# Two steps' values and two steps' scores in one TensorE run for the last two blocks, a second buffer for the turned probabilities, six ring buffers, and a new table of due times

## The chip, the core and the metric

The kernel runs on one core of one Trainium2 chip. The metric is the device time of one execution in microseconds (us). Engines are named as in the profile: PE is TensorE, DVE is VectorE, ACT is ScalarE, POOL is GpSimd, SP is SyncE, which here only issues DMA transfers.

## What is computed

A banded attention over 8 batches, 8 heads, 576 positions and a head size of 64, followed by a feed-forward layer with 512 inputs, 2048 hidden units and 512 outputs over all 4608 tokens:

```python
scores = scale * np.matmul(q, k.transpose(0, 1, 3, 2))
mask = (rel >= 0) & (rel < window)          # rel = query position - key position, window = 64
attn = softmax(np.where(mask, scores, -1e9))
x = np.matmul(attn, v)                      # heads joined: 4608 x 512
h = x @ w_in                                # 512 -> 2048
g = np.where(h >= 1, h, np.where(h <= -1, 0.0, (h + 1) ** 2 / 4))
out = g @ w_out                             # 2048 -> 512
```

## The kernel before, in words

Attention goes in 36 steps of 128 queries, 4 per tile of 512 tokens. A step has four parts. `att_scores` on PE (line 422, in short S) multiplies queries and keys of all heads: 64 small matmuls in the trace from step 5 on. `att_masked`, `att_exp`, `att_inverse` and `att_normalize` on DVE, ACT and sometimes POOL make probabilities of them. For steps from 5 on `att_turn` (DVE, line 491), `att_write` and `att_read` (SP, lines 502 and 505) transpose these: they are written to one tensor `moved` in DRAM and read back into one buffer, `turned` (named `ptd` in the profile). `att_values` on PE (line 535, in short V) multiplies them by the values: 32 small matmuls in the trace.

The feed-forward layer of the first three tiles runs straight: `ffn_in` (line 1139) and `ffn_out` (line 1185). The other six tiles go in three blocks of two tiles (`add_super`), each by a scheme with 7 products where plain blocking needs 8. `ffn_product` (line 914) makes 56 products of 6 matmuls for the first layer, `out_product` (line 1000) 56 more for the second. The scheme's weight operands lie in DRAM (`kept`), and each product reads one of them, 256 KB, through a ring of SBUF buffers (`ring_load`, line 894; `ring=7` in `BUFS`). Its input operands are sums and differences of attention outputs, made in `add_build` (lines 570 and 606) when both steps r and r+4 of a block are there, so the steps go in the order `A_ORDER` = 0, 4, 1, 5, 2, 6, 3, 7.

Nothing is ordered by hand. Every piece of work is put into a list (`plan.add`) with a key, a cost for each engine that could do it, what it needs and which buffers it takes. `Plan.run` then lays the pieces out one by one: on each engine the piece that can start first, among those about equally early the one with the lowest key. Keys come from the constants at the top of the file. What comes out is a fixed order of instructions on each engine; on the chip each engine goes through its own in that order and waits where an operand is missing. SP too: a transfer that waits holds up all transfers behind it.

Before the change a late step puts on PE one piece, V of an older step and S of its own (`do` in `add_step`); the last two steps' V of a block stand alone, and so do the first two S. The attention of a block runs on PE between the products of the block before.

Of the kernel before, what the change touches and what calls it, by code (L numbers as in the profile page):

```python
# [10 lines left out]
F32 = mybir.dt.float32  # L11
F32R = mybir.dt.float32r
# [30 lines left out]
E_SPAN = 5.91  # L43
E_LEAD = 17.1
W_LEAD = -23.43
W_FIRST = (41.07, 11.15, 26.87, -10.88, -31.72)
W_STEP = 25.17
L_LEAD = -2.38
W_LATE = (3.63, -16.39, 9.21, 20.15, 0.56)
V_LATE = 14.51  # L50
W0_KEY = -103.61
FIRST_LOAD = 0, (0,)
M_LATE = 5.76
W0_STEP = 8.68
FINE = 4
NWARM = 8
A_FIRST = (-100.35, -96.85, -96.18, -80.14)
A_NEXT = 10.78
A_STEP = 5.01
A_SPAN = 18.65  # L60
A_LEAD = 5.32
O_LAG = 2.91
# [11 lines left out]
B_DUE = (4.53, -27.23, 1.18)  # L74
B_STEP = 13.93
B_FIRST = -15.42
A_END = 2.75
V_PE = 1270
NORM = dict(Pool=800, DVE=480), dict(DVE=610)
G_LATE = (11.92, 0.97, -5.01, 12.64, 1.72)  # L80
D_LATE = (-2.36, 0.62, 26.98, 2.89, 13.75, 21.44)
TURN = 965, 1500
# [4 lines left out]
SUM_KEEP = 880  # L87
V_LATE_2 = 43.01
LAND = 800
WRITE = 1140  # L90
BACKLOG = 2500
MOVED = 3700
PATIENCE = dict(ACT=300, DVE=0, Pool=303, PE=0, SP=0)
BUFS = dict(qt=2, kt=2, vt=4, ps_a=2, sm=2, ptd=3, pt2=1, x=2, u=2, ps_h=2, a=2, gh=2, gl=2, acc=4, o=2, tmp=2)
BUFS.update({n: 1 for n in ("xtmp", "xs0", "xs1", "xs2", "xs3", "xs4", "xs5", "X", "Y")}, raw=4, ring=7, op=5)

# [4 lines left out]
S_LATE = 5.22  # L101
S_PACE = 47.29
O_CHANGE = (-1.18, 7.84, 12.31)
EARLY_2 = 3.64
A_SUPER = ((10.49, 4.41), (12.01, 4.44))
A_ORDER = (0, 4, 1, 5, 2, 6, 3, 7)
BUILD = (-17.42, 29.27)
# [5 lines left out]
R_LEAD = -10.33  # L113
R_LOAD = 370
L_DVE = 4, 6, 8
G_LEAD = (9.32, -1.73, 0.08, 4.82)
OP_LEAD = 45.65
D_LEAD = 1.02
# [6 lines left out]
class Plan:  # L125
# [29 lines left out]
    def run(self):  # L155
# [22 lines left out]
        for _ in self.work:  # L178
            best = None
            for e in engines:  # L180
# [12 lines left out]
                if could:  # L193
                    until = min(could)[0] + PATIENCE[e]
                    c = min((c for c in could if c[0] <= until), key=lambda c: c[1:])
                    best = c if best is None else min(best, c)
# [26 lines left out]
def banded_attention_then_ffn(ctx: ExitStack, tc: tile.TileContext, q, k, v, w, masks, out, out_t, dims):  # L223
# [26 lines left out]
    idt = const.tile([P, P], F32, name="idt")  # L250
    make_identity(nc, idt)
    msk = const.tile([P, 3, WIN], F32, name="msk")
# [89 lines left out]
    def w_low(g):  # L342
        t = ws[g]
        nc.vector.tensor_tensor(out=t[:, :, 1], in0=us[g], in1=t[:, :, 0].bitcast(F32), op=ALU.subtract)
# [3 lines left out]
    def add_weights(f, units):  # L348
# [6 lines left out]
        x = add(key - W_LATE[1], dict(ACT=act, DVE=67 + 1.05 * m), lambda e: w_top(g, e), [xr])  # L355
        x = add(key - W_LATE[2], dict(DVE=join), lambda e: w_join(g), [x])
        x = add(key - W_LATE[3], dict(ACT=high, DVE=30 + .6 * m), lambda e: w_high(g, e), [x])
        x = add(key - W_LATE[4], dict(DVE=low), lambda e: w_low(g), [x], gives=[("u", xr)])
# [145 lines left out]
    def att_read():  # L504
        nc.sync.dma_start(out=turned, in_=moved.rearrange("i k r j n -> (k r) i (j n)"))
# [19 lines left out]
    def att_values(s, pool):  # L525

        vt, pt = [vts.pop((s, i)) for i in range(2)], [ptd[pt_of(s, h)] for h in range(2)]
        vals[s] = ps = banks_of_heads(pool)
        for p in range(NP):
            for i in range(2):  # L530
                n = slice(i * QB, (i + 1) * QB)
                for h in range(2):
                    c = (2 * p + h) * D
                    w_ = turned[:, i].rearrange("p (j g n) -> p j g n", j=2, n=SQ)[:, :, h * NP + p] if s >= SOON else pt[h][:, p, n]
# [92 lines left out]
    def add_build(u, r, due, x0, x1):  # L627
# [3 lines left out]
        xs = i0  # L631
        for j in range(1, 4):
            xs = add(due, tt(2 * SB), lambda e, j=j: x_sums(r, j, e), [xs], shared=True)
        end = []
        for k in range(6):
            n = 4 * SB if k == 0 else 2 * SB
            after, slot, takes = [xs], f"xs{k}", []
# [9 lines left out]
            x = add(due, tt(n), lambda e, k=k: x_low(r, k, e), [x] + end, gives=gives, shared=True)  # L647
            end = [x]
            x_of[u, k].append(x)

    def add_step(t, i):
# [21 lines left out]
        xq = add(lk, dict(SP=390), lambda e: load_q(s), takes=["qt"], moves=packets(P, 4 * DM))  # L673
        xk = add(lk, dict(SP=480), lambda e: load_k(s) if s else None, takes=["kt"], moves=packets(P, 6 * DM) if s else None)
        vk, vc = lk + (V_LATE_2 if late else V_LATE), 450 if s < SOON else 640
        xv = add(vk, dict(SP=vc), lambda e: load_v(s, 0), takes=["vt"], moves=packets(P, 4 * DM), behind=last["v"])
        xw = add(vk, dict(SP=vc), lambda e: load_v(s, 1), takes=["vt"], moves=packets(P, 4 * DM), behind=[xv])
        last["v"] = [xw]
# [25 lines left out]
        if s < SOON:  # L704
            for h in range(2):
# [8 lines left out]
                x = add(due + D_LATE[3], dict(DVE=420), lambda e, h=h: att_inverse(s, h), [x])  # L714
                x = add(due + D_LATE[4], NORM[1], lambda e, h=h: att_normalize(s, h, e), [x], shared=True)
# [21 lines left out]
        else:  # L737
            dk = key if s >= JOIN else min(key + E_SPAN, soon(s) - E_LEAD)
            due = [dk + B_DUE[0], dk + B_DUE[0] + B_DUE[2]]
            x = [add(due[h], dict(DVE=LOWEST), lambda e, h=h: att_masked(s, h), [xs, last["m"]], gives=[(ps, xs, h)]) for h in range(2)]  # L740
            x = [add(due[h], dict(ACT=EXP[1]), lambda e, h=h: att_exp(s, h, False), [x[h]]) for h in range(2)]
            x = add(due[1], dict(DVE=430), lambda e: att_inverse(s, BOTH), x)
# [670 lines left out]
```

## Time and profile before

| | us |
|---|---|
| median of 3 runs (834.3 to 835.08) | 834.69 |
| profiled execution, its own time | 835.11 |
| its span, first to last instruction | 833.2 |
| PE busy / DVE busy / ACT busy / POOL busy | 817.4 / 673.7 / 520.8 / 229.8 |

The first 25.75 us of the span hold the first four attention steps; the first `ffn_in` starts then. Up to 62 us the weights come in from DRAM. At 334 us the first block's products begin, at 829 us the last matmul ends.

### The profile page before, as it was taken

What the parts mean: (1) busy time and instruction counts of PE and PEld (TensorE: products, weight loads), DVE (VectorE), ACT (ScalarE), POOL (GpSimd) and SP (SyncE); (2) the same over time, 40 slices, a digit from 0 to 9 for tenths busy, and PEclk for the clock granted to TensorE, in tenths of its full rate; (3) what the DMA queues carried; (4) which work ended last, traced back from release to release, by engine and by line L of the source; (5) the groups of instructions that cost most, each with busy time, mean ns of one, the idle gap of its engine ahead of it and who ended that gap; (6) DMA issues with size and microseconds to landing.
All of it is one profiled execution on the core that took longest, in us unless ns stands there. A gap on an engine that the chain in (4) does not pass through costs nothing.

```text
span 833.2 us, 18542 instructions
## 1 busy us (share of the span) xinstructions
PE 817.4 (98%) x6588; PEld 670.0 (80%) x6588; DVE 673.7 (81%) x1551; ACT 520.8 (63%) x1287; POOL 229.8 (28%) x244
## 2 busy tenths in 40 slices
PE   5999999999999999999999999999999999999998
PEld 4778888888887888888888788888888888888886
DVE  6999976467765699599899995888999948888964
ACT  7889955555666656667875563777655535566442
POOL 1000043346645744556223321140133101100100
PEclk8999999999999999999999999999999999999999
DMA  9993389976778985899978979899787786666675
GB/s 350 421 418 107 103 273 358 358 241 207 220 254 267 286 258 159 285 313 341 332 221 278 311 240 341 276 293 311 221 240 230 251 252 193 193 194 194 202 218 162
DMA packets 151900, 216.06 MB, mean 259 GB/s; under 512 B 11905, under 2 KB 75265, under 8 KB 151809
## 3 DMA queue, kind: packets, MB, share of 16 engines
q1 hardware_dynamic: 151520, 213.97, 79.6%
q8 instruction: 52, 0.85, 0.4%
q10 hardware_dynamic: 288, 0.92, 0.3%
q14 instruction: 40, 0.32, 0.1%
HBM read 163.72 MB, written 51.12 MB: 258 GB/s over the span
## 4 chain that ended last, share of the span: by engine, by line
PE 87%; DMA 6%; DVE 5%; ACT 1%; issue 0%; SPq 0%; ACTq 0%; DVEq 0%
PE acc L1000 23%; PE acc L1185 14%; PE ps_h L1139 14%; PE ps_h L914 14%; PE acc L914 14%; PE ps_a L422 3%; DMA kt<-in_k 2%; PE ps_h L535 1%; PE acc L535 1%; PE ps_a L535 1%; DMA vt<-in_v 1%; DMA ptd<-moved 1%; DVE g L978 1%; DVE op L991 1%; DMA raw<-in_w 1%; DMA moved<-sm 1%
## 5 line engine op out<-in xcount | busy, mean ns | idle before, releaser
L1000 PE MATMUL acc<-op,wts 128*128 128x512 f32 x576 | 138.4, 391 | 0.0
L294 ACT CAST op<-g 128x512 fp32r<-128x512 f32 x125 | 77.7, 622 | 84.4 <-PE acc L1000 49.3
L1139 PE MATMUL ps_h<-xh,wts 128*128 128x512 f32 (+1 forms) x424 | 129.9, 373 | 0.0
L1000 PEld LDWEIGHTS acc<-op,wts 128*128 128x128 f32 x576 | 107.6, 188 | 22.9
L1185 PE MATMUL acc<-wts,gh 128*128 128x512 f32 x384 | 120.3, 395 | 0.0
L991 DVE TENSOR_TENSOR op<-g,op 128x512 fp32r<-128x512 f32 x119 | 87.6, 737 | 17.7 <-ACT op L294 17.0
L465 ACT ACTIVATE sm<-sm,nm 128x96 f32<-128x96 f32 x248 | 89.5, 363 | 14.3 <-DVE nm L445 12.5
L914 PE MATMUL ps_h<-wts 128*128 128x512 f32 x360 | 92.1, 391 | 0.0
L914 PE MATMUL acc<-wts 128*128 128x512 f32 x360 | 91.9, 390 | 0.0
L1139 PEld LDWEIGHTS ps_h<-xh,wts 128*128 128x128 f32 x424 | 77.5, 188 | 15.2 <-issue 0.3
L1185 PEld LDWEIGHTS acc<-wts,gh 128*128 128x128 f32 x384 | 70.7, 188 | 15.4
L1154 ACT ACTIVATE a<-a 128x512 f32<-128x512 f32 (+1 forms) x129 | 79.5, 617 | 3.9
L914 PEld LDWEIGHTS acc<-wts 128*128 128x128 f32 x360 | 67.4, 188 | 14.6 <-issue 0.3
L914 PEld LDWEIGHTS ps_h<-wts 128*128 128x128 f32 x360 | 67.2, 188 | 14.6
L1139 PE MATMUL ps_h<-xl,wts 128*128 128x512 f32 (+1 forms) x212 | 78.6, 371 | 0.0
L1185 PE MATMUL acc<-wts,gl 128*128 128x512 f32 x192 | 74.9, 390 | 0.0
L1149 ACT ACTIVATE a<-g 128x512 f32<-128x512 f32 x96 | 60.3, 629 | 19.9 <-DVE g L929 15.1
L1161 DVE SCALAR_TENSOR_TENSOR g<-a,g 128x512 f32<-128x512 f32 x96 | 67.9, 714 | 5.4 <-ACT a L1154 5.2
L1171 POOL TENSOR_TENSOR gl<-a,gh 128x512 fp32r<-128x512 f32 (+1 forms) x34 | 46.8, 1378 | 59.8 <-ACT gh L1166 55.0
L1149 ACT ACTIVATE a<-ps_h 128x512 f32<-128x512 f32 (+1 forms) x53 | 29.5, 557 | 53.4 <-PE ps_h L1139 53.0
L1161 DVE SCALAR_TENSOR_TENSOR a<-a,ps_h 128x512 f32<-128x512 f32 (+1 forms) x53 | 33.6, 634 | 34.8 <-ACT a L1154 34.5
L978 DVE TENSOR_TENSOR g<-g 128x512 f32<-128x512 f32 x82 | 56.9, 708 | 0.4
(142 smaller groups left out, 1529.4 us busy)
## 6 DMA issues: line engine op xcount, KB each, us to landing
wts<-kept SPq DMA_DIRECT2D x240, 256.0 KB, 3.5
vt<-in_v SPq DMA_DIRECT2D x72, 256.0 KB, 5.7
ptd<-moved SPq DMA_DIRECT2D x31, 512.0 KB, 4.6
kt<-in_k SPq DMA_DIRECT2D x35, 384.0 KB, 6.0
kept<-wts SPq DMA_DIRECT2D x48, 256.0 KB, 4.6
gh<-kept SPq DMA_DIRECT2D x48, 256.0 KB, 3.5
gl<-kept SPq DMA_DIRECT2D x48, 256.0 KB, 3.7
raw<-in_w SPq DMA_DIRECT2D x12, 1023.8 KB, 12.3
```

The costliest lines, as they stand in the source:

```text
L294: nc.scalar.copy(dst, src)
L465: nc.scalar.activation(t, t, AF.Exp, bias=nm[:, g:g + 1], scale=-1.0, accum_out=den[:, g:g + 1])
L914: nc.tensor.matmul(ps, lhsT=r[:, part, cp], rhs=x_op(k, xp)[:, cp], start=j in (0, 1, 3, 4) and i == 0 and cp == 0, stop=j in (1, 2, 5, 6) ...
L978: engine[eng].tensor_tensor(out=g[:, out], in0=g[:, a], in1=g[:, b], op=op)
L991: engine[eng].tensor_tensor(out=low, in0=g_of(n)[:, of], in1=high.bitcast(F32), op=ALU.subtract)
L1000: nc.tensor.matmul(opened[b][m], lhsT=r[:, part, m], rhs=op[xp], start=j in (0, 1, 3, 4) and i == 0 and n == 0, stop=j in (1, 2, 5, 6) and ...
L1139: nc.tensor.matmul(ps, lhsT=wts[f, 0][:, part, c * P:(c + 1) * P], rhs=x[:, c, r], start=(c == 0 and j == 0), stop=(c == NP - 1 and j == 2),)
L1149: nc.scalar.activation(gs[t, f, r.start][0], phs[t, f, r.start], AF.Relu, bias=0.5, scale=0.5)
L1154: nc.scalar.activation(a, a, AF.Square)
L1161: nc.vector.scalar_tensor_tensor(out=ps if t >= PLAIN else a, in0=a, scalar=1.0, in1=ps, op0=ALU.min, op1=ALU.max)
L1171: engine[eng].tensor_tensor(out=g[2], in0=g[0], in1=g[1].bitcast(F32), op=ALU.subtract)
L1185: nc.tensor.matmul(acc[t, i][:, n], lhsT=g[:, sub], rhs=wts[f, 1][:, part, n], start=(q == 0 and j == 0), stop=(q == NF - 1 and j == 2 and ...
```

## The change

For the last two blocks (u = 1, 2) a new function `add_pairs` takes the place of `add_step`. It treats steps r and r+4 together. Five runs stand in a block: S S, then three times V V S S (the values of the pair before, the scores of the next), then V V. Within a run the second and later parts have a key lowered by 2000 (`NOW`), so that PE goes on with them. A run may start when both pairs of queries and keys, both turned probabilities and the values of the pair are there. The turned probabilities get a second buffer (`pt2=2`), made of two tiles that the early stages no longer need; a read into it is issued as two transfers. The ring falls from seven buffers to six, since one of those tiles was its seventh slot. `moved` in DRAM stays one tensor.

The rest moves work by rules and numbers: nearly all constants at the top are new; `add_build` and `add_outs` state what each single sum needs instead of all before it; the two halves of a weight sum are written to DRAM by transfers of their own; the low halves of the weights, the normalisation and the low halves of the first tile's gates may now go to POOL. The core of the diff:

```diff
-V_PE = 1270
+NOW = -2000
+URGENT = 900
-BUFS = dict(qt=2, kt=2, vt=4, ps_a=2, sm=2, ptd=3, pt2=1, ...
+BUFS = dict(qt=2, kt=2, vt=4, ps_a=2, sm=2, ptd=3, pt2=2, ...
-BUFS.update(..., raw=4, ring=7, op=5)
+BUFS.update(..., raw=4, ring=6, op=5)
...
-    def att_read():
-        nc.sync.dma_start(out=turned, in_=moved.rearrange("i k r j n -> (k r) i (j n)"))
+    def att_read(s, x):
+        pt_slot[s] = b = plan.slots[x, "pt2"][0]
+        src = moved.rearrange("i k r j n -> (k r) i (j n)")
+        if b == 0:
+            nc.sync.dma_start(out=turned, in_=src)
+        else:
+            for i, t in enumerate(turned_of(b)):
+                nc.sync.dma_start(out=t, in_=src[:, i])
...
-        x = add(key - W_LATE[4], dict(DVE=low), lambda e: w_low(g), [x], gives=[("u", xr)])
+        x = add(key - W_LATE[4], dict(DVE=low, Pool=200 + 2.15 * m), lambda e: w_low(g, e), [x], gives=[("u", xr)], shared=True)
...
+    def add_pairs(u):
+        end, apart = A_PAIR[u - 1]
+        before = []
+        for r in range(5):
+            key = block_key(u, 0) - end - apart * (4 - r)
+            pj = "acc" if key < block_key(u - 1, 1) else "ps_h"
...
+            for j, (s, xt_, v) in enumerate(before):
+                after = [xs] if j else needs + [y for _, a, b in before for y in (a, *b)]
+                xs = add(
+                    now if j else key, dict(PE=V_RUN[j] + (150 if r == 4 and j else 0)), lambda e, s=s: att_values(s, "ps_a"), after,
+                    takes=["ps_a"] + room * (j == 0), gives=[("pt2", xt_), ("vt", v[0]), ("vt", v[1])],
+                )
...
+            x1 = add(
+                now if before else key, dict(PE=S_RUN[not before]), lambda e, s=steps[0], pj=pj: att_scores(s, False, pj), ...
+            x2 = add(
+                now, dict(PE=S_RUN[2]), lambda e, s=steps[1]: att_scores(s, False, "ps_a"), [x1], takes=["ps_a", "ps_a"], ...
...
-        for i in A_ORDER:
-            add_step(PLAIN + 2 * u, i)
+        if u:
+            add_pairs(u)
+        else:
+            for i in A_ORDER:
+                add_step(PLAIN, i)
```

How this moves instructions is seen in the order on the engines. The first place is PE among the first block's products: one of its runs. `ptd` are turned probabilities, `vt` values, `kt` and `qt` keys and queries, `ps_h` and `acc` PSUM banks of products. Before:

```order
L914 MATMUL acc<-wts 128x512 x6
L535 MATMUL acc<-ptd,vt 64x64 x16
L422 MATMUL ps_a<-kt,qt 32x96 x32
L914 MATMUL ps_h<-wts 128x512 x6
L914 MATMUL acc<-wts 128x512 x6
```

And after:

```order
L996 MATMUL acc<-wts,gl 128x512 x6
L559 MATMUL ps_a<-ptd,vt 64x64 x32
L430 MATMUL acc<-kt,qt 32x96 x32
L430 MATMUL ps_a<-kt,qt 32x96 x32
L996 MATMUL ps_h<-wts 128x512 x6
```

Six V S runs, two S and two V alone of a block have become five runs. Between the runs of the first of the two blocks stand 42, 20, 21 and 19 products, of the second 22, 21, 27 and 19. Behind the first stage PE has, elsewhere, as many runs of attention of each kind as before, at other places.

The second place is SP around such a run. `wts`, `gh` and `gl` read from `kept` are the ring's buffers. Before, the loads of one step stand between ring loads:

```order
L894 DMA wts<-kept_94 128x512
L505 DMA ptd<-moved 128x2x512
L390 DMA qt<-in_q 128x512
L394 DMA kt<-in_k 128x768
L400 DMA vt<-in_v 128x1x512
L894 DMA gh<-kept_93 128x512
L400 DMA vt<-in_v 128x1x512
L894 DMA gl<-kept_94 128x512
```

After, eight loads stand in one row, and the writes and reads of the two steps follow each other between ring loads:

```order
L408 DMA vt<-in_v 128x1x512 x3
L398 DMA qt<-in_q 128x512
L402 DMA kt<-in_k 128x768
L398 DMA qt<-in_q 128x512
L402 DMA kt<-in_k 128x768
L408 DMA vt<-in_v 128x1x512
```

```order
L510 DMA moved<-sm 64x3x256 x2
L976 DMA wts<-kept_102 128x512
L976 DMA wts<-kept_103 128x512
L976 DMA gh<-kept_104 128x512
L528 DMA ptd<-moved 128x512 x2
L976 DMA gl<-kept_105 128x512
L976 DMA wts<-kept_106 128x512
L976 DMA wts<-kept_107 128x512
L976 DMA wts<-kept_100 128x512
L510 DMA moved<-sm 64x3x256 x2
```

There are five such rows of eight. Each stands behind exactly six ring loads more than products have run, so with the ring full, and its first transfer waits for the run's first V.

The third place is PE in the first stage, from the first `ffn_in` on (`xh`, `xl` inputs, `idt` or `early` the identity for transposes of probabilities). Before, three groups of four transposes stand in a row:

```order
L1139 MATMUL ps_h<-xh,wts 128x256
L520 MATMUL ps_a<-idt,sm 128x128 x12
L535 MATMUL ps_a<-ptd,vt 64x64 x16
```

After, four stand between the first and the second twelve `ffn_in` matmuls, and the rest behind the second:

```order
L1221 MATMUL ps_h<-xh,wts 128x256
L543 MATMUL ps_a<-early,sm 128x128 x8
L559 MATMUL ps_a<-ptd,vt 64x64 x16
L543 MATMUL ps_a<-early,sm 128x128 x4
L1221 MATMUL ps_h<-xh,wts 128x256
```

In the first microseconds SP now issues the second step's queries and keys ahead of the second weight load, and the order of PE up to the first `ffn_in` is the same.

## Rows read from the trace of the kernel before

**Rows 1.** Page, part 1: engine, busy us (share of the span), instructions.

```profile
PE 817.4 (98%) x6588; PEld 670.0 (80%) x6588; DVE 673.7 (81%) x1551; ACT 520.8 (63%) x1287; POOL 229.8 (28%) x244
```

**Rows 2.** Windows, first two stages: length, busy by engine, granted clock, DMA share, GB/s.

```profile
0.00:25.75 25.75, 16.72 (x232) 13.33 (x233) 18.44 (x42) 18.91 (x58) 2.91 (x16) 0.87 0.94 365
25.75:62.00 36.25, 34.49 (x332) 28.96 (x329) 34.46 (x81) 31.25 (x95) 0.00 (x0) 1.00 1.02 419
```

**Rows 3.** Waits of PE, whole span: total us, times, longest.

```profile
PE ps_h L520 <- DVE den L476: 4.0, 1, 4.0
...
PE acc L422 <- DMA kt<-in_k: 1.4, 1, 1.4
PE ps_h L535 <- DMA ptd<-moved: 0.8, 1, 0.8
...
PE ps_a L535 <- DMA ptd<-moved: 0.6, 1, 0.6
```

**Rows 4.** Timeline of PE, one joined run (start us, us, what).

```profile
342.18 1.52 PE L914 MATMUL ps_h<-wts 128*128 128x512 f32 x6
343.63 1.15 PE L535 MATMUL acc<-ptd,vt 128*64 128x64 f32 x32
344.71 1.00 PE L422 MATMUL ps_a<-kt,qt 64*32 64x96 f32 x64
345.63 1.67 PE L914 MATMUL acc<-wts,gh 128*128 128x512 f32 x6
347.14 1.55 PE L914 MATMUL ps_h<-wts,gl 128*128 128x512 f32 x6
348.53 1.52 PE L914 MATMUL acc<-wts 128*128 128x512 f32 x6
349.89 1.52 PE L914 MATMUL ps_h<-wts 128*128 128x512 f32 x6
```

**Rows 5.** Timeline of PE, one V alone and one S alone.

```profile
460.44 0.39 PE L1000 MATMUL acc<-gh,wts 128*128 128x512 f32 x1
460.76 1.15 PE L535 MATMUL ps_a<-ptd,vt 128*64 128x64 f32 x32
461.84 1.66 PE L1000 MATMUL acc<-op,wts 128*128 128x512 f32 x6
463.33 0.39 PE L1000 MATMUL acc<-op,gh 128*128 128x512 f32 x1
...
501.81 1.52 PE L1000 MATMUL acc<-op,wts 128*128 128x512 f32 x6
503.27 0.99 PE L422 MATMUL ps_a<-kt,qt 64*32 64x96 f32 x64
504.19 1.65 PE L1000 MATMUL acc<-op,wts 128*128 128x512 f32 x6
505.68 0.40 PE L1000 MATMUL acc<-gh 128*128 128x512 f32 x1
```

**Rows 6.** Groups by form on PE, from 62 us: count, busy us, mean ns.

```profile
L422 PE MATMUL ps_a<-kt,qt 64*32 64x96 f32 x1920 | 29.9, 248 | 0.0
L535 PE MATMUL ps_h<-ptd,vt 128*64 128x64 f32 x416 | 15.0, 225 | 0.8 <-DMA ptd<-moved 0.8
```

**Rows 7.** Timeline (first) and chain that ended last: the first block's last step.

```profile
452.77 1.00 PE L422 MATMUL ps_a<-kt,qt 64*32 64x96 f32 x64
...
467.94 0.89 DVE sm L491
...
469.53 2.87 DMA moved<-sm
...
472.45 5.08 DMA ptd<-moved
```

**Rows 8.** Line 894, the ring loads from 340 to 415 us: issue to landing.

```profile
DMA to landing us min/median/max: 2.7/5.0/7.3
```

**Rows 9.** Windows, attention alone on PE (columns as in rows 2).

```profile
19.40:25.75 6.35, 6.35 (x137) 5.14 (x137) 6.18 (x13) 5.22 (x13) 0.00 (x0) 0.92 1.05 424
```

More of the change, by code (lines that the diff above doesn't have):

```diff
@@ L630, in add_build @@
         i0 = add(due, tt(2 * SB), lambda e: x_sums(r, 0, e), [x0, x1], takes=["xtmp"] + ["u"] * first, shared=True)
[L631 to L634, printed above, removed]
+        i2 = add(due, tt(2 * SB), lambda e: x_sums(r, 1, e), [i0], shared=True)
+        i1 = add(due, tt(2 * SB), lambda e: x_sums(r, 2, e), [i0], shared=True)
+        i3 = add(due, tt(2 * SB), lambda e: x_sums(r, 3, e), [i1], shared=True)
+        lows = []
         for k in range(6):
             n = 4 * SB if k == 0 else 2 * SB
-            after, slot, takes = [xs], f"xs{k}", []
+            after, slot, takes = [(i0, i1), (i2,), (i3,), (x0, x1), (x0, x1), (x0, x1)][k], f"xs{k}", []
+            after = list(after)
             if (u, k) in x_of:
@@ new lines, in add_loads @@
+    def add_loads(s, lk, vk, vc):
+        xq = add(lk, dict(SP=390), lambda e: load_q(s), takes=["qt"], moves=packets(P, 4 * DM))
+        xk = add(lk, dict(SP=480), lambda e: load_k(s) if s else None, takes=["kt"], moves=packets(P, 6 * DM) if s else None)
+        xv = add(vk, dict(SP=vc), lambda e: load_v(s, 0), takes=["vt"], moves=packets(P, 4 * DM), behind=last["v"])
+        xw = add(vk, dict(SP=vc), lambda e: load_v(s, 1), takes=["vt"], moves=packets(P, 4 * DM), behind=[xv])
+        last["v"] = [xw]
+        return xq, xk, xv, xw
@@ new lines, in add_take @@
+    def add_take(u, i, due, xo, pv):
+        s, r = starts[PLAIN + 2 * u] // SB + i, i % 4
+        after, takes = [xo], []
+        if i < 4:
+            takes = ["raw"]
+            if u == 0:
+                after.append(x_in[PLAIN - 2])
+        else:
+            after.append(raw_of[u, r])
+        x = add(due, dict(ACT=485, DVE=608), lambda e: x_take(s, i, e), after, takes=takes, gives=[(pv, xo)])
+        if i < 4:
+            raw_of[u, r] = x
+        else:
+            add_build(u, r, max(due, 0), raw_of[u, r], x)
@@ L738, in add_step @@
             dk = key if s >= JOIN else min(key + E_SPAN, soon(s) - E_LEAD)
[L739 to L742, printed above, removed]
[L743 to L751 removed]
+            x = add_turn(s, xs, dk, [(ps, xs, h) for h in range(2)], ("sm", xs))
+            due = dk + B_DUE[1]
+            first = taken = ready = [x]
             gives = [("pt2", taken[0])]
@@ L758, in split @@
             if t >= PLAIN:
[L759 to L772 removed]
+                add_take((t - PLAIN) // 2, i, due, xo, pv)
                 return
@@ L1252, in add_gate @@
         xl = add(
-            key + late[4], low, lambda e: ffn_low(t, f, r, e), [xh], takes=["gl"], gives=[("a", xa)], shared=t > 0,
+            key + late[4], low, lambda e: ffn_low(t, f, r, e), [xh], takes=["gl"], gives=[("a", xa)], shared=True,
         )
```

221 lines of the change are left out of this document (128 added, 93 removed).

## The prediction

> **What bounds the kernel now.** I read the page's list of engines first, then windows by stage, then PE's own waits, then single stretches of its timeline. PE is busy for 98% of the span [rows 1], but a busy PE says little, so the question is whether it ever waits and what it pays besides the big matmuls. In the first 25.75 us it is busy for 16.72, and in the weight stage up to 62 us for 34.49 of 36.25; 1.76 are idle there [rows 2]. Behind that, the only two waits of PE that reach half a microsecond are 0.8 and 0.6 us, both for the turned probabilities [rows 3]. So from 62 us on the time is the sum of what PE issues. What can fall is the start, the 1.76 us, the 1.4 us of waits and the price of attention itself.
>
> That price is read from when the products go on. Two products of six matmuls start 1.36 us apart (348.53 and 349.89), so one matmul costs 0.227 us. Around a joined run of V and S, three products start at 342.18, 345.63 and 347.14 and the fourth at 348.53: 6.35 us where three products alone take 4.08, so the run costs 2.27 [rows 4]. A V alone: 2.89 us from 460.44 to 463.33 with seven matmuls (1.59) costs 1.30. An S alone: 3.87 us from 501.81 to 505.68 with twelve (2.72) costs 1.15 [rows 5]. Joining V and S thus saves 0.18 once.
>
> **The pairs.** A block of before has six joined runs, two S and two V alone: 6 x 2.27 + 2 x 1.15 + 2 x 1.30 = 18.5 us. After, it has S S, three times V V S S, and V V. No row shows a V behind a V or an S behind an S, so I bound the added one. From above by the full distance of starts: V to S 1.08 and S to the next product 0.92 [rows 4]. These contain a change of kind at their end. From below without it: V's 32 matmuls end 1.15 us after the first start and one lasts 225 ns, so the last starts after 0.925; with one more of the 31 inner steps (0.03 each) an added V costs 0.955. For S, 1.00 less 248 ns is 0.752, and with an inner step of 0.012 it is 0.764 [rows 4, 6]. V V S S then costs 2.27 + 1.72 to 2.00 = 3.99 to 4.27 against 4.54 for two joined runs; S S saves 0.23 to 0.39 and V V 0.22 to 0.35. A block saves 1.3 to 2.4 us, both blocks 2.5 to 4.8. An added step keeps the kind of matmul, which is what the lower price describes, so I take **-4.3**.
>
> **The start.** The order on PE up to the first `ffn_in` stays, but the second step's scores waited 1.4 us for keys [rows 3] that are now asked for ahead of a weight load. The 4.0 us wait for the first normalised probabilities [rows 3] shrinks only as far as its own chain on DVE and ACT starts earlier. Behind it, PE's idle 1.76 us lay mostly among the twelve transposes that stood in one row; now twelve `ffn_in` matmuls stand between the first four and the rest. Both could go whole, -3.2, or new weights could come too late for the new order, which I bound by the same idle time again, +1.8. POOL takes low halves of weights that DVE made; no wait of PE hung on those. I take somewhat over half, **-2.0**.
>
> **Old waits later.** The 0.8 and 0.6 us [rows 3] stood where a single step's read came too late. The new order has none of those places; their like is priced below. Half of them, **-0.7**; between -1.4 and 0.
>
> **The ring.** Six buffers cover 6 x 1.36 = 8.16 us of products, where seven covered 9.52. Ring loads between 340 and 415 us landed 5.0 us after issue in the median and 7.3 at most [rows 8]. With seven buffers that left 2.2 us at worst and PE waited for none; with six, 0.86. Ahead of five runs stand eight transfers in a row (four values, two queries, two keys: 2.3 MB, where one step's four have 1.15). At the 419 GB/s of the busiest stage [rows 2] the added 1.15 MB take 2.7 us. If all of it stood before a ring load that was already at the worst, it would land 7.3 + 2.7 - 8.16 = 1.9 us late, five times: +9. Below, nothing: the ring is full when the run begins, PE takes none of it during some 4.0 us of run, and the eight are issued as V and S free their buffers, so most of the burst moves inside the run. That last is nearest to the order, so **+0.7**.
>
> By the Trainium skill, DMA: Bandwidth & Descriptors, section Queues, rings and completion order, work of one issuing queue starts in its order on each DMA engine. All of these transfers are SP's, so by this rule the burst delays each ring load behind it by all that is left of it. The trace agrees so far as the spread of 2.7 to 7.3 us to landing shows loads that wait behind others [rows 8]; by the rule at its worst the sum would have the +9, by the median landing of 5.0 nothing.
>
> **The pair's chain.** What is queued behind a late read is everything on PE: V waits, and the products behind it. In the first block's last step S starts at 452.77, the turn ends at 468.83 (467.94 + 0.89), 16.1 us later; the write takes 2.87 and the read 5.08 [rows 7]. A pair's second write waits for the first read, since `moved` is one tensor. At the pace of before, the first V of a pair is ready 16.1 + 8.0 = 24.1 us after the first S and the second 32.1. The order leaves, with n products between two runs, two S (1.84) and one V (0.955) and 1.36 n: 28.6 us for n = 19, 30.0 for 20, 31.4 for 21. Over the gaps 20, 21, 19 and 22, 21, 27, 19 the second V would wait 2.1 + 0.7 + 3.5 + 0 + 0.7 + 0 + 3.5 = 10.5 us in all. With a turn 3.5 us sooner it never waits. In the 16.1 us lie DVE's sums of the block, done before the step because nothing needed it yet, so a step that is due sooner can be done sooner. I take **+1.2**, nearer to nothing than to 10.5.
>
> **The sum.** Against the profiled 835.11 us (span 833.2 and 1.9 around it): -4.3 - 2.0 - 0.7 + 0.7 + 1.2 = -5.1, so 830.0. The median of before lies 0.4 under its profiled run, so I forecast 829.6. DVE, 81% busy [rows 1], gets no new work and stays off the bound but for the chain above. The other new dependencies, on single sums and transfers, let DVE, ACT and POOL work earlier; with PE waiting for next to nothing they are worth what the waits above are worth and no more.
>
> **Rivals.** *The pair's second read is late at each gap* (the other side): the 10.5 in place of 1.2 gives 838.9. For it: one `moved`, and two round trips of 8.0 in one gap. Against it: the slack inside the 16.1. It decides from the point at which the turn comes about 10 us later than the best, that is, no sooner than before: then 5.1 + 1.2 are eaten. Chance 0.10. *Ring loads late behind each burst*: half of the +9, 4.5 in place of 0.7, gives 833.4. For it: the worst landing leaves 0.86 us. Against it: a full ring at the run's start. Chance 0.10. *The start gives nothing and an added step costs its full distance* (-2.5, 0): 833.4, chance 0.09. *Everything falls into place*: start -3.2, pairs -4.8, waits -1.4, no new ones: 825.3, chance 0.07.
>
> *The clock falls in the longer runs.* A run of small matmuls now lasts 4.0 us where it lasted 2.0. If these did not keep the clock up, the six runs of 4.0 and what follows each would go at 1.2 GHz; doubling the runs alone costs +24: 853. Against it: from 19.40 to 25.75 PE did attention alone, and the granted clock rose there to a mean of 0.92 [rows 9], and stayed 1.00 behind it [rows 2]. Chance 0.02. By the Trainium skill, TensorE: Matmul & The Clock Gate, section Part 1: The HAM clock gate, the granted clock follows how busy the engine has recently been; by that rule a run without a gap keeps it, and the trace agrees.
>
> **How the numbers follow.** My forecast has 0.62: 829.6, itself between 826 and 833. A difference of 0.2%, 1.7 us, is about what a measurement of this kernel can tell from none, so faster means under 833.0. All of the forecast, the best case and a half of the ring's and the start's cases lie there: 0.79. Within 0.2%: the rest of these two and an edge of the pair's rival, 0.11. Slower: 0.10. The range goes from 825.0, which holds the best case, up to 834.5, which holds the ring's and the start's rivals.
>
> **What would show it.** A run V V S S costs 4.0 us by the same reading of products; products stay 1.36 us apart; the first `ffn_in` starts before 25 us, and idle time up to 62 us falls under 1.2. Waits of PE for reads of `moved` (n = 19 first), or for `kept` behind a burst, would show the rivals. I am wrong if such waits sum to over 5 us or the start comes later.

## The result, and the profile after

The changed kernel takes 846.09 us (median of 6 runs, 842.45 to 849.21), the kernel before in the same set 834.88 (834.15 to 835.73): ratio 1.0132, 95% interval 1.0105 to 1.0159. It is 1.3% slower, 11 us, where 5 us faster were forecast. Its profiled execution took 849.21 us (span 847.2). That is its slowest run, so a second trace was taken, of an execution of 844.20 (span 842.4); both are used below.

The first two windows, which answer to [rows 2]:

```profile
0.00:25.75 25.75, 19.75 (x232) 15.53 (x232) 17.61 (x36) 16.08 (x51) 7.79 (x20) 1.00 0.95 365
25.75:62.00 36.25, 34.00 (x418) 28.97 (x410) 33.62 (x89) 32.03 (x103) 7.10 (x6) 0.95 1.02 417
```

PE is idle for 2.25 us between 25.75 and 62 us, where it was for 1.76, and the clock is 0.95 there (2.04 and 1.00 in the second trace). The 1.00 of the first row says less than it seems: the second step's S took 1.99 us in that window and 1.10 before, so PE ran at about half speed for a part of it that the column doesn't show. The first `ffn_in` starts at 26.58 us (25.98 in the second trace, 25.75 before).

The first transposes, in the kernel before and in the second trace:

```profile
16.54 2.88 PE L520 MATMUL ps_h<-idt,sm 128*128 128x128 f32 x12 [4.00 <-DVE den L476]
```

```profile
15.07 3.23 PE L543 MATMUL ps_h<-early,sm 128*128 128x128 f32 x12 [3.92 <-POOL sm L492]
```

PE's own waits in the profiled run, which answer to [rows 3]:

```profile
PE ps_h L996 <- DMA wts<-kept: 2.6, 1, 2.6
PE ps_h L543 <- POOL sm L492: 2.5, 1, 2.5
PE ps_a L430 <- issue: 2.4, 2, 1.2
...
PE ps_h L559 <- DMA ptd<-moved: 1.9, 4, 0.9
PE acc L1082 <- DMA wts<-kept: 1.8, 2, 1.3
...
PE ps_a L559 <- DMA vt<-in_v: 1.3, 1, 1.3
PE ps_h L1221 <- DVE xl L572: 1.1, 1, 1.1
PE acc L430 <- ACT o L302: 1.0, 1, 1.0
PE ps_h L996 <- DMA gh<-kept: 1.0, 2, 0.7
...
PE ps_a L559 <- DMA ptd<-moved: 0.6, 1, 0.6
```

Products (lines 996 and 1082) wait for ring loads (`kept`), which none did before. An early `ffn_in` matmul waits for `xl`, the low halves of its inputs, which is new too. V (line 559) waits more often for the turned probabilities. And S (line 430) pauses twice for 1.2 us with no releaser that the profile knows ("issue"); both pauses lie inside the second S of a V V S S.

The price of a run, from PE's timeline around the first V V S S, as in [rows 4]:

```profile
401.35 1.52 PE L996 MATMUL acc<-wts,gl 128*128 128x512 f32 x6
402.80 2.09 PE L559 MATMUL ps_a<-ptd,vt 128*64 128x64 f32 x64
404.82 0.93 PE L430 MATMUL acc<-kt,qt 64*32 64x96 f32 x60
...
406.53 1.66 PE L996 MATMUL ps_h<-wts 128*128 128x512 f32 x6
408.02 1.52 PE L996 MATMUL acc<-wts 128*128 128x512 f32 x6
409.38 1.52 PE L996 MATMUL ps_h<-wts 128*128 128x512 f32 x6
```

From 401.35 to 409.38 three products start, 8.03 us where they alone take 4.08: the run costs 3.95. Read in the same way, S S costs 1.88 and V V 2.24 where nothing is late. A block's attention costs 1.88 + 3 x 3.97 + 2.24 = 16.0 us in place of 18.5: having fewer seams, the changes between products and attention, gives 5.0 us in both blocks.

What eats this is read by two sums, for every kernel below. **Stalls**: from the first product on, all distances of over 0.38 us between the starts of two neighbouring product matmuls, each less 0.227 (0.227 is what one matmul takes; the sum also counts matmuls at half clock, 0.427 apart). **Late**: what runs of S and V from 180 us on cost above their price without waits (1.17, 1.31, 2.25 for both, 1.88, 2.24, 3.98), before and behind the first product.

| profiled execution | stalls | late before | late behind |
|---|---|---|---|
| before, 835.11 | 0 | 0.9 | 0.8 |
| after, 849.21 | 7.8 | 5.7 | 3.8 |
| after, second trace, 844.20 | 7.7 | 4.2 | 2.7 |

The second trace: 7.7 of stalls, 5.2 of added lateness, less 5.0 of seams, make +7.9 of the +9.1 us; the rest lies in the start and in small pieces. So the seams gave what they should, and the stalls and the late runs took over twice as much. All nine stalls of the second trace are of a product that starts 0.13 to 0.14 us after its ring load landed, or that the profile puts down to one.

The late runs before the first product are mostly single steps of the first block, for which the forecast had no term. The chain of waits of the profiled run there:

```profile
297.95 6.92 DMA moved<-sm
...
305.30 3.08 DMA ptd<-moved
...
309.18 4.11 DMA moved<-sm
...
313.34 3.53 DMA ptd<-moved
...
317.00 1.15 PE ps_h L559 x32
```

Write, read, write, read, one behind the other through the one tensor `moved`, and then V, which starts late.

SP's queue shows what the same chain does to the transfers behind it (total us, times, longest):

```profile
SPq L510 <- DMA ptd<-moved: 23.5, 15, 3.7
SPq L525 <- DMA moved<-sm: 14.3, 15, 3.5
SPq L528 <- DMA moved<-sm: 12.2, 10, 3.2
```

And in the kernel before:

```profile
SPq L505 <- DMA moved<-sm: 26.4, 17, 2.8
...
SPq L502 <- DMA ptd<-moved: 7.8, 5, 1.9
```

At 15 writes SP stood for the read of the step before, 23.5 us in all, and at 25 reads for their own write, 26.5 us. The reads stood as long before the change; what has tripled is the waits of the writes. Ring loads stand in that queue too.

### The profile page after: what moved, and what is told of

Read it like the earlier page. It is cut to its first block, busy times and chain, and to the rows that moved or that the text cites. A ratio compares the mean times of both kernels' runs of the same rounds, so it can differ in the third digit from the quotient of the medians.

```text
span 847.2 us, 18550 instructions
## 1 busy us (share of the span) xinstructions
PE 821.5 (97%) x6588; PEld 673.5 (80%) x6588; DVE 674.3 (80%) x1573; ACT 520.5 (61%) x1285; POOL 214.4 (25%) x224
## 4 chain that ended last, share of the span: by engine, by line
PE 83%; DMA 10%; DVE 2%; SPq 1%; ACT 1%; issue 1%; POOL 0%; ACTq 0%; DVEq 0%
PE acc L1082 24%; PE ps_h L1221 14%; PE acc L1267 13%; PE ps_h L996 13%; PE acc L996 12%; DMA wts<-kept 3%; PE ps_a L559 3%; DMA ptd<-moved 2%; PE ps_a L430 2%; DMA moved<-sm 2%; DMA gh<-kept 1%; DMA gl<-kept 1%; PE ps_h L559 1%; DMA kept<-o 1%; PE acc L430 0%
## 5 line engine op out<-in xcount | busy, mean ns | idle before, releaser
L1082 PE MATMUL acc<-op,wts 128*128 128x512 f32 x540 | 130.5, 391 | 1.4 <-DMA wts<-kept 1.3
L1082 PEld LDWEIGHTS acc<-op,wts 128*128 128x128 f32 x540 | 100.7, 188 | 24.1 <-ACT op L302 1.6
L1073 DVE TENSOR_TENSOR op<-g,op 128x512 fp32r<-128x512 f32 x115 | 80.7, 708 | 20.2 <-ACT op L302 19.2
L996 PE MATMUL ps_h<-wts 128*128 128x512 f32 x336 | 85.8, 391 | 2.6 <-DMA wts<-kept 2.6
L996 PE MATMUL acc<-wts 128*128 128x512 f32 x336 | 85.3, 389 | 0.0
L996 PEld LDWEIGHTS ps_h<-wts 128*128 128x128 f32 x336 | 62.7, 188 | 16.6 <-DVE g L1243 3.0
L1236 ACT ACTIVATE a<-a 128x512 f32<-128x512 f32 (+1 forms) x118 | 72.5, 615 | 3.4
L996 PEld LDWEIGHTS acc<-wts 128*128 128x128 f32 x336 | 63.1, 188 | 13.1
L1060 DVE TENSOR_TENSOR g<-g 128x512 f32<-128x512 f32 x84 | 58.6, 722 | 0.5
```

The costliest lines, as they stand in the source:

```text
L996: nc.tensor.matmul(ps, lhsT=r[:, part, cp], rhs=x_op(k, xp)[:, cp], start=j in (0, 1, 3, 4) and i == 0 and cp == 0, stop=j in (1, 2, 5, 6) ...
L1060: engine[eng].tensor_tensor(out=g[:, out], in0=g[:, a], in1=g[:, b], op=op)
L1073: engine[eng].tensor_tensor(out=low, in0=g_of(n)[:, of], in1=high.bitcast(F32), op=ALU.subtract)
L1082: nc.tensor.matmul(opened[b][m], lhsT=r[:, part, m], rhs=op[xp], start=j in (0, 1, 3, 4) and i == 0 and n == 0, stop=j in (1, 2, 5, 6) and ...
L1236: nc.scalar.activation(a, a, AF.Square)
```

## The experiments

Theory A: six ring buffers are too few. Theory B: a pair's two round trips through one `moved` are late. Theory C: the new table of due times costs time before the first product. Later D (all round trips through one tensor, block one's too), E (ring loads are late because they stand behind a round trip that waits in SP's queue) and F (not the number of buffers but a ring load's place in SP's queue). All results together, with the sums of the one trace of each; ratios are against the kernel before on the same chip (its medians there 835.2 to 836.8):

| run | us | ratio, interval | stalls | late before | late behind |
|---|---|---|---|---|---|
| e7 changed kernel again | 845.09 | 1.0106 [1.0063, 1.0148] | 7.7 | 4.2 | 2.7 |
| e4 before, six buffers | 842.85 | 1.0085 [1.0072, 1.0098] | 5.1 | 1.3 | 3.2 |
| e2 seven buffers, new plan | 842.06 | 1.0071 [1.0055, 1.0087] | 1.7 | 5.1 | 7.0 |
| e1 loads spread | 858.09 | 1.0274 [1.0258, 1.0289] | 15.1 | 3.2 | 3.7 |
| e3 lag 1500 | 863.58 | 1.0338 [1.0321, 1.0356] | 15.7 | 18.4 | 11.5 |
| e5 seven, two tensors, new plan | 851.95 | 1.0182 [1.0142, 1.0222] | 4.5 | 11.3 | 5.7 |
| e6 two tensors, new plan | 855.40 | 1.0201 [1.0152, 1.0250] | 10.2 | 12.1 | 3.5 |
| e8 table of before | 861.26 | 1.0318 [1.0303, 1.0333] | 12.2 | 0.2 | 30.1 |
| e10 two tensors, order kept | 838.49 | 1.0039 [1.0025, 1.0053] | 6.1 | 0.4 | 1.8 |
| e11 seven, order kept | 846.97 | 1.0141 [1.0099, 1.0183] | 9.2 | 5.3 | 1.1 |
| e12 both, order kept | 842.04 | 1.0089 [1.0071, 1.0108] | 8.6 | 1.2 | 1.3 |
| e13 both, loads one place up | 835.82 | 0.9995 [0.9983, 1.0008] | 3.5 | 0.5 | 4.0 |
| e14 seven, loads one place up | 843.60 | 1.0086 [1.0061, 1.0112] | 2.1 | 6.0 | 7.6 |
| e15 two tensors, loads spread | 847.81 | 1.0141 [1.0124, 1.0159] | 13.5 | 0.4 | 1.9 |
| e16 before, two tensors | 835.59 | 0.9996 [0.9984, 1.0007] | 0 | 0.8 | 1.9 |
| e17 e13, reads one load later | 838.61 | 1.0020 [1.0006, 1.0035] | 4.2 | 1.0 | 4.6 |
| e18 e10, reads one load later | 840.66 | 1.0051 [1.0031, 1.0070] | 5.9 | 0.9 | 3.6 |

A tenth of a per cent in a ratio is 0.84 us. In e3, e5, e6, e8 and e17 the stalls hold 3.4, 1.6, 1.4, 3.6 and 1.4 us of matmuls at half clock, which are no waits of their own.

**First set: one part undone each.** The plan is made anew in e2 to e4; e1 changes only SP's order.

e4, the kernel before with the change's ring:

```diff
-..., raw=4, ring=7, op=5)
+..., raw=4, ring=6, op=5)
```

> The kernel before with six ring buffers in place of seven, made in the way of the change; no pairs, no other constants. The kernel before had a least slack of 0.14 to 0.5 us between a ring load's landing and its product with seven buffers. Theory A in the form that six buffers alone do it: 1.36 us less on each tight load, stalls of 4 to 9 us, time 839 to 844. Theory that the burst of a pair is needed as well: single steps load 1.15 MB at once, not 2.3, stalls of 0 to 2 us, time 835 to 837.

7 us slower, as theory A has it: the kernel before stalls at ring loads for 5.1 us once it has six buffers, without any pair. So the loss is not the pairs' burst alone. (Its plan was made for six, so its loads stand at other places too.)

e2, the changed kernel with a seventh buffer:

```diff
-..., raw=4, ring=6, op=5)
+..., raw=4, ring=7, op=5)
+            elif i == 6:
+                ring_slots[i] = const.tile([P, DM], F32R, name="wts", tag="rounded")
```

> The changed kernel with a seventh ring buffer (two small constant tiles merged and reused once the early work is over); the order is made anew with it. Theory A (ring of six as a whole): from free to use there are 8.16 us in place of 6.8, stalls of ring loads fall from 9 to about 1 us, time 837 to 839. Theory of the burst alone (eight transfers in a row hold up a ring load by up to 2.7 us whatever the number of buffers): stalls fall by 1.36 us for each of the larger ones, to some 3 us, time 839 to 841. Theory B (the round trips of a pair): no change, 845 to 847.

Stalls fall from 7.7 to 1.7, as A has it, but only 4 us show, less than A's 7 to 9: late values rise from 6.9 to 12.1. PE now comes sooner to values that were not there any sooner.

e1, a pair's loads taken apart:

```diff
+                if u > 1 or r:
+                    plan.later.update(x for some in loads for x in some)
...
+            if i in self.rings and self.waiting:
+                some, on = self.waiting.pop(0)
+                some(on)
```

> The changed kernel, but the eight q, k and v loads ahead of a pair (all pairs except the first) stand in SP's queue one behind each following ring load instead of eight in a row; the orders of PE, DVE, ACT and POOL stay. Theory A (the loss is mostly the ring: six buffers, and ring loads held up by the burst): the stalls of some 9 us six products behind nearly every run shrink to 1 to 3, time 837 to 840. Theory B (the loss is the pair's two round trips through the single tensor for the turned probabilities): those stalls are 3.7 us in the changed kernel and nothing here touches them, time 845 to 847. Theory C (six buffers are too few even without a burst): stalls stay above 5 us and only move, time 842 to 845.

No theory had this: 12 us slower. For twelve products behind the run at 396.96 PE doesn't stall (the second trace of the changed kernel has 0.33 us there at the sixth), then it does. SP's timeline there:

```profile
417.03 0.42 SPq L985 DMA_DIRECT2D wts<-kept  x1
417.55 0.38 SPq L985 DMA_DIRECT2D gh<-kept  x1
418.49 0.32 SPq L985 DMA_DIRECT2D gl<-kept  x1
421.64 1.24 SPq L517 DMA_DIRECT2D moved<-sm  x2
422.98 0.55 SPq L985 DMA_DIRECT2D wts<-kept  x1
```

From 418.81 to 421.64 SP stands at a write of turned probabilities, and ring loads wait behind it. The burst, in a row, fell into the run, during which PE takes no product; spread out it takes SP's time beside the products and then meets the round trip.

e3, the planner's lag:

```diff
-TURN = 965, 100
+TURN = 965, 1500
```

> The changed kernel with the planner's cost behind a turn set back from 100 to 1500 ns, all else as changed; the order is made anew. Theory C1 (the planner believes that a turned tensor comes back 1.4 us sooner than it does, so V stands too early): the late V at 201, 286, 308, 317 and 337 us (about 5 us in all) and in the pairs (3.7 us) fall by half or more, time 840 to 843. Rival: the order is full of other constants fitted to the 100, so a V that stands later pushes products against a bound elsewhere: 845 to 852. If the waits are the chip's own (round trips of 13 us in a row, with steps 10 us apart), moving V only trades one stall for another: 845 to 847.

The rival, and by more than it gave. Waits of PE (first row of the list):

```profile
PE ps_a L559 <- DMA ptd<-moved: 12.0, 4, 6.9
```

The other constants fit the 100; a single number of the table can't be read as a cause.

**Second set: the round trips.** e5 and e6 give `moved` a second tensor, used by turns, and plan anew.

```diff
-    moved = dram.tile([2, SQ, 4, 2, 2 * NP * SQ], F32, name="moved")
+    moved = [dram.tile([2, SQ, 4, 2, 2 * NP * SQ], F32, name=f"moved{a}") for a in range(2)]
...
-        last["d"] = last["t"] = [x]
+        last[seq[s] % 2] = last["t"] = [x]
```

> The changed kernel with seven ring buffers and with two tensors for the turned probabilities, used by turns, so that a step's write no longer waits for the read of the step before it. The run with seven buffers alone took 842.1 us and its values still waited 5.4 us for turned probabilities (five places from 314 us on), with 1 us of half clock behind one of them. Theory D (what the ring gave back went into the round trips through one tensor): these waits go, time 834 to 837. Rival (the turns themselves come too late, from DVE): they stay, 841 to 843.

> The changed kernel with two tensors for the turned probabilities, ring of six as it is. Theory D with theory A: the round trips lose their 4 to 9 us, but PE comes to the ring loads sooner, and half of the gain goes into longer ring stalls: 840 to 844. If the two costs add without acting on each other: 837 to 840. If the round trips cost nothing: 845 to 847.

Both are slower than the changed kernel, against every expectation. The new plan put the first block's last V behind the first S S, and the first product waited for an operand that ACT could only make after it (e5, PE's longest wait):

```profile
PE ps_h L1000 <- ACT wts L303: 5.6, 1, 5.6
```

So these two tell of the plan and not of the tensors. From here on the order was kept.

e7 is the changed kernel itself (its trace is the second one above).

> The changed kernel as it is, for a second trace of it: the profiled execution took 849.2 us, 3 us above its median. Theory: the 1.3 us gap and the two us of half clock right behind the first ffn_in are not in every execution, and the ring stalls (9 us) and the late values (9 us) are. Time 844 to 848.

As expected in time. The half clock behind the first `ffn_in` is gone, a gap of 1.1 us there is not, and the late values are 6.9 us in that trace and not 9: they vary from one execution to the next, as the total does (842.51 to 849.56).

e9 issues writes and reads from POOL:

```diff
-        nc.sync.dma_start(out=moved.rearrange("i k r j n -> (i k) r j n")[:, j:j + 3, j], in_=t)
+        nc.gpsimd.dma_start(out=moved.rearrange("i k r j n -> (i k) r j n")[:, j:j + 3, j], in_=t)
```

> The changed kernel, but the writes and reads of the turned probabilities are issued by POOL, at the same places of the program, and no longer stand in SP's queue. In the changed kernel SP stands still for 24 us at 15 writes (for the read before) and for 27 us at 25 reads (for the write), and ring loads behind them are issued up to 3.2 us after their buffer came free. Theory E (ring loads are late because they stand behind a round trip that waits in SP's queue): the ring's stalls fall from 9 to some 2 us; time 838 to 842, if POOL's own rows (low halves, normalising) behind a waiting issue don't make PE wait; with that, 842 to 848. Theory A without it (the window of six alone): stalls stay, 845 to 848.

908.57 us is the median of four, 905.84 that of the three without an execution of 2079 us (ratio of the three 1.0837 [1.0781, 1.0893]). The trace is of that execution, in which a product's matmul took 828 ns on average and not 391, so it doesn't show where the 60 us of the others went. Their mean granted clock was 0.963 to 0.967, where e7's was 0.993 to 0.996: an estimate from these shares (0.029 of 905 us) puts some 26 us of the 60 down to half clock, and what made PE fall to it is not shown. Inconclusive.

**Third set: the order of every engine kept to the row.** e10 has the two tensors, but planned as if there were one.

> The changed kernel with two tensors for the turned probabilities, but planned as if there were one, so that every engine keeps its order to the row (the run before this with two tensors was planned anew, and its new order brought a wait of 5.6 us of its own). Theory D (the round trips through one tensor are late): the late values of block one, some 4 us, and of the pairs, 2 to 4 us, go; what PE gains it meets again in part at ring loads: 839 to 842. Theory that SP's queue holds ring loads behind a write that waits for the read before: the ring's stalls fall too, by half: 835 to 839. Rival (the turns come late, not the tensor): 844 to 846.

7.6 us faster than the changed kernel, a little better than D alone had it. What PE still waits for `moved` in the whole kernel:

```profile
PE ps_h L560 <- DMA ptd<-moved: 0.2, 1, 0.2
```

Late values fall from 6.9 to 2.2, stalls from 7.7 to 6.1 (not by half), and no write of the turned probabilities waits for a read any more. Theory D is shown.

e11 has seven buffers used in turn, planned as six, and e12 both.

```diff
-        r = ring_slot(plan.slots[x, "ring"][0])
+        r = ring_slot(loaded[0] % 7)
+        loaded[0] += 1
```

> The changed kernel with seven ring buffers used in turn, but planned as if there were six, so that every engine keeps its order. Theory A (from free to use six buffers leave 6.8 us, too little for loads that are issued up to 3.2 us late and land up to 7.4 us after issue): the ring's stalls, 7 to 9 us, fall under 1, late values grow by 1 to 3: 838 to 841. Theory E (SP's queue alone): a ring load's issue is still up to 3 us late but it has 1.36 us more, stalls of 2 to 3 us: 840 to 843.

> Both: seven buffers and two tensors, with the changed kernel's order. If the ring and the round trips are the loss, and one only hid behind the other, this takes both away: 832 to 836, with the changed start and its pairs as they are. If the first 340 us hold a loss of their own: 836 to 839.

Both came above every range. Theory A, that a buffer more is enough, falls: a seventh at the same order gives nothing (846.97), and with two tensors it is worse than without (842.04 against 838.49; why it is worse, no run shows). What e2 gained in stalls it had with a plan made for seven. SP's timeline at one pair, changed kernel (second trace) first and then e11:

```profile
430.50 0.32 SPq L976 DMA_DIRECT2D wts<-kept  x1
431.48 1.90 SPq L408 DMA_DIRECT2D vt<-in_v  x3
433.47 0.54 SPq L398 DMA_DIRECT2D qt<-in_q  x1
434.06 0.43 SPq L402 DMA_DIRECT2D kt<-in_k  x1
434.58 0.39 SPq L398 DMA_DIRECT2D qt<-in_q  x1
435.02 0.42 SPq L402 DMA_DIRECT2D kt<-in_k  x1
435.49 1.14 SPq L408 DMA_DIRECT2D vt<-in_v  x1
436.73 1.33 SPq L976 DMA_DIRECT2D wts<-kept  x2
```

```profile
430.17 0.32 SPq L980 DMA_DIRECT2D gh<-kept  x1
432.51 1.90 SPq L409 DMA_DIRECT2D vt<-in_v  x3
...
436.52 1.21 SPq L409 DMA_DIRECT2D vt<-in_v  x1
437.77 0.63 SPq L980 DMA_DIRECT2D gl<-kept  x1
```

For 5.2 us (431.48 to 436.63) SP does nothing but issue a pair's eight loads, and no ring load is issued from 430.82 to 436.73. With seven buffers the load at 437.77 goes into a buffer that had been free for 6.3 us, and is no earlier: it stands behind the eight. (The changed kernel's load at 436.73 goes out 0.9 us after its buffer came free.)

e8 takes every number of the table from before, with pairs and seven buffers.

> The changed code with its pairs and seven ring buffers, planned with the table of before wherever the table of before has the number (the costs and due times of the start, of single steps, gates, sums, the ring). Theory C (the new table of due times costs some 4 us before the first product and the pairs are a gain by themselves): 833 to 838. Rival (the pairs stand where they do only with the new table, so the old one brings reads or builds that come late): 842 or more.

The rival: values in pairs wait (9.4 us, longest 6.8). The pairs need their table. For C there is more here: e8 differs from e2 in the table alone, and late values before the first product are 0.2 against 5.1, so the new table makes those. The early first product (332.57, 340.21 in e2) says less, since one S S and 12 matmuls of `ffn_out` that e2 has ahead of it stand behind it.

**Fourth set: places in SP's queue.** e13 and e14 issue each ring load from the eighth on where the one before it stood; e13 is e12 with this edit, e14 is e11.

```diff
+        ahead = len(fired) + (len(fired) > 6)
+        while loaded[0] < min(ahead, len(loads)):
+            l, u, n, j = ring_keys[loads[loaded[0]]]
+            r = ring_slot(loaded[0] % 7)
```

> Seven buffers, two tensors, every engine's order as changed, but from the eighth on each ring load is issued at the place in SP's queue where the one before it stood: one product sooner, in front of the eight loads of a pair where it stood behind them. Theory F (the place in SP's queue is what counts, the buffer only allows it): the ring's stalls of some 8 us (842.0 without the shift) fall under 2, time 833 to 836. Theory that loads land late because the transfers themselves collide: stalls stay above 5, 839 to 842.

> The same shift with seven buffers but one tensor for the turned probabilities (847.0 without the shift). Theory F: ring stalls fall from 9 to 2 or 3, late values stay (7 us in the first 340 us and the pairs): 839 to 842. If writes that wait for a read in SP's queue are the larger part of the ring's delay, less: 842 to 845.

F is shown: by this shift alone 842.04 becomes 835.82, and stalls fall from 8.6 to 3.5, though not under the 2 that was expected. With one tensor 846.97 becomes 843.60 (e14; the intervals overlap). The time is that of e14's second case, but not for its reason: stalls fall from 9.2 to 2.1, as in the first, and late values rise from 6.4 to 13.6. One place, SP and PE of e12 first, then of e13:

```profile
631.48 0.88 SPq L981 DMA_DIRECT2D wts<-kept  x2
635.21 1.30 SPq L512 DMA_DIRECT2D moved<-sm  x2
...
637.25 0.40 SPq L981 DMA_DIRECT2D gh<-kept  x1
...
642.37 1.40 PE L1087 MATMUL acc<-op,gh 128*128 128x512 f32 x5 [1.60 <-DMA gh<-kept]
```

```profile
631.67 0.32 SPq L989 DMA_DIRECT2D gh<-kept  x1
634.24 1.24 SPq L514 DMA_DIRECT2D moved<-sm  x2
...
639.63 1.53 PE L1097 MATMUL acc<-op,gh 128*128 128x512 f32 x6
```

In e12 the load of `gh` is issued behind a write for which SP stood from 632.4 to 635.2, and PE waits 1.60 us for it. In e13 it is issued 2.6 us ahead of the write, and PE doesn't wait.

e15 spreads the loads again, with two tensors; e16 gives the kernel before two tensors.

> Six buffers, two tensors, and a pair's eight loads spread one behind each following ring load. Spread loads with one tensor took 858: stalls right behind the runs went, but new ones came behind writes and reads of turned probabilities in SP's queue. Theory F: with two tensors a write no longer waits for a read, so the spread is worth what it takes away behind the runs: 834 to 838 against 838.5 without the spread. Rival (two DMA streams beside the products are too much for six buffers): 842 to 852.

> The kernel before, order kept, with two tensors for the turned probabilities. It waits 1.4 us for them in all: 833.5 to 834.5 if these waits came from the one tensor, 835 if from late turns.

e15: the rival's time. Writes no longer wait for reads, but ring loads still come late where the spread loads meet the round trip (stalls 13.5). e16: no change that can be told; what writes wait for reads in the kernel before (7.8 us of SP's time) costs it nothing that shows.

e17 and e18 put each read of a pair behind the next ring load.

> As the run with seven buffers, two tensors and ring loads one place up (835.8 us), but each read of a pair's turned probabilities stands behind the next ring load in SP's queue, which then needn't wait for the write to land. Theory F (places in SP's queue): the ring's stalls of 3.5 us fall to 2, reads are at most 0.5 us later: 833.5 to 835.5. Rival (the late reads cost V as much): 835.5 to 838.

> Six buffers, two tensors (838.5 us), and each read of a pair's turned probabilities behind the next ring load. In that kernel SP stood 24 us at reads that waited for their write, and ring stalls were 6 us, about half of them behind such waits. Theory F: stalls fall to 3 or 4 us: 835.5 to 837.5. Rival: a read waits until the next ring buffer comes free, up to 1.36 us, and V is as much later: 838 to 841.

Both rivals (e17 0.6 us above its range), some 2 us slower each. Late values rise (e17 from 4.5 to 5.6, e18 from 2.2 to 4.5) and stalls hardly fall (without half clock e17 from 3.5 to 2.8, e18 from 6.1 to 5.9). No version beat the kernel before; e13 equals it.

## Why the prediction was wrong

- **The pairs (-4.3)**: right, slightly under-sized. V V S S costs 3.95 to 4.05 where nothing in it is late, at or just under the cheap end of the 3.99 to 4.27; both blocks give 5.0. An added step keeps the kind of matmul and pays little.
- **The ring (+0.7, bounded by +9)**: the step that failed. It measured 7.7 to 7.8, near the bound. Three things in it were wrong. "Six buffers cover 8.16 us": a buffer isn't free while its own product runs, so five products, 6.8 us, lie between free and next use. The burst was priced in bytes (2.7 us at 419 GB/s), where what counts is SP: 5.2 us of issuing, in which no ring load goes out. And the round trips' waits in SP's queue were left out of this term, though the text says that a transfer that waits holds up all behind it. "Most of the burst moves inside the run" was half right: in the second trace 2.7 of the 5.2 us of issuing fall into the run that begins at 430.40; taken out of there, the burst cost 12 us more (e1). And e4 has it without pairs: 7.1 us for six buffers and the plan made for them. The rule of the Trainium skill weighed there (DMA: Bandwidth & Descriptors, section Queues, rings and completion order) is about transfers already in the DMA engines; what the runs show lies ahead of it, in the order in which SP issues them.
- **The pair's chain (+1.2)**: right, and the late reads came where the forecast looked first, in a V V behind 19 products: 0.6 us in the profiled run and 0.7 in the second trace. But behind the first product runs are late by 3.8 and 2.7 us, against 0.8 before, and the larger part is what no term had: the pauses inside the second S of a pair, 2.4 and 1.3 us. In every trace looked at for this (both of the changed kernel, e10 and e13) a 16 KB transfer of PE's instructions starts 2.1 to 2.8 us into such a run, 0.9 to 1.6 us ahead of the pause. That PE goes through a joined run faster than its instructions come is argued from that, not shown: a transfer at the like place of another run brought no pause, and no run tests it.
- **Old waits later (-0.7)**: wrong in sign. The like of them came in the first block, which still goes in single steps: 4.2 to 5.7 us against 0.9. That the new table moved them there is shown by e8 beside e2 (0.2 against 5.1), that they hang on the one `moved` by e10 (0.4 left), and that the kernel before had room for it by e16; that the lag of 100 ns made them is not shown (e3 changed too much at once).
- **The start (-2.0)**: wrong. The wait of 1.4 us for keys went, as forecast, while PE's 4.0 us wait for DVE became one of 2.5 us for POOL (3.9 in the second trace). So in the second trace the first transposes start at 15.07 us, 1.47 sooner. Of that 0.72 went where more of the matmuls behind them ran at half speed (V took 1.98 us, 1.61 before), and 0.66 into a wait of V for values. Behind the first `ffn_in` the transposes wait for 0.5 us where they waited for 1.2, but the matmul behind it waits 1.1 us for `xl`. The forecast let only new weights come late; what came late was `xl` and the values.
- **The rivals**: "ring loads late behind each burst" had the right mechanism at half its size; at the size measured it alone turns -5.0 into +2.7. The clock didn't fall in the longer runs: from 62 to 835 us it was 1.00 in both traces. Both signs of being wrong that the prediction named came: waits for `kept` sum to 6.0 us in the profiled run, and the start is later.

Where the 5.0 us went: of e13's 838.33 (its profiled run), against 835.11, stalls have +3.5, added lateness +2.8, the seams -5.0; the +1.9 that is left lies in the start and in small pieces. With neither stall nor lateness and the start of before it would come near 830; no run shows that kernel.

What stays open: what pauses PE inside the second S; why a seventh buffer made e12 slower than e10; what the transfers issued by POOL did (e9); and why single executions of the changed kernel spread over 7 us.

## What to carry to other kernels

In a queue that issues in order, price a burst by its issue time and by the waits of everything in the row, not by its bytes; a prefetch ring is as good as the place of its loads in that queue, and another buffer gives nothing until the loads move up with it. Count a ring's cover from the moment a buffer is free to its next use, one product less than the number of buffers. A scratch tensor that every step writes and reads back is a buffer of one: look at it before the steps are put closer together. And where a fitted table sets the order, undo a part with the order kept, or the new plan will answer in its place.

## What the runs showed of the hardware

After an idle PE the clock can fall: in e5 PE waited 2.82 us and then ran at a granted clock of 0.50, the lower level of 1.2 GHz (window columns as in [rows 2]).

```profile
242.80:245.50 2.70, 2.67 (x6) 2.17 (x7) 0.90 (x2) 1.98 (x4) 1.99 (x3) 0.50 0.39 139
245.50:250.00 4.50, 4.50 (x20) 3.71 (x19) 1.78 (x4) 0.23 (x1) 0.05 (x1) 0.96 0.69 208
```

Six matmuls started in these 2.7 us, where at 0.227 twelve would: the wait cost half as much again. The length of the wait alone doesn't decide: in e17 a wait of 2.29 us for a ring load was followed by 3.4 us at 0.50, while behind waits of 2.6 us (the changed kernel's profiled run) and 1.9 us (V V at 496 us in e14) the products went on at 1.00. What tells them apart, no run here shows. Not expected either: a pair's eight loads took SP 5.2 us to issue, 0.65 each, where a ring load alone took 0.32; two ring loads right behind them took 0.6 each too.
